# A gated linear recurrence followed by a multiplicative feed-forward: masks, the exchanged v, and the quarters of the array

## The chip, the core and the metric

The kernel runs on one core of one Trainium2 chip. The metric is device time in microseconds (us) for the whole program. The engines are named as in the profile: PE is TensorE (PEld its weight loads), DVE is VectorE, ACT is ScalarE, POOL is GpSimd, SP is SyncE, which here only starts DMAs. An L with a number is a line of the kernel before, unless the text says that it is a line of the changed kernel.

## The reference

Per batch and head (4 x 8, 768 positions, 48 values) a state of 48 x 48 decays by `alpha`, takes in `k v`, and is read by `q`. The result, as a matrix of 3072 x 384, goes through a feed-forward whose two input products are multiplied together.

```
for t in range(S):
    state = alpha[:, :, t, :, None] * state + einsum('bhd,bhe->bhde', k[:, :, t], v[:, :, t])
    y[:, :, t] = einsum('bhd,bhde->bhe', q[:, :, t], state)
x = y.transpose(0, 2, 1, 3).reshape(B * S, H * D)          # 3072 x 384
a = x @ w1                                                 # 384 x 1024
b = x @ w2
h = a * b @ w3                                             # 1024 x 1024
out = h @ w_out                                            # 1024 x 384
```

The activations are float32; the weights arrive as 64-bit floats and are converted on the chip.

## The kernel before

**Tiling.** The 24 chunks are 4 batches of 6 chunks of 128 positions. A head's 48 values are padded to 64, so the 8 heads make 4 pairs (`j`), and a pair fills 128 partitions: head 2j lies in rows 0 to 63 (`i = 0`), head 2j+1 in rows 64 to 127 (`i = 1`). TensorE's array is used in parts: a product with 48 or 64 rows and 64 columns takes a quarter of it, named here (row half, column half). Which row half depends on where the operands lie, which column half on the partitions of the result. Plain float32 products appear in the profile as two matmul records each (20 chunks x 8 products are 320 records at L474); transposes and the split products of the feed-forward appear as one.

**Steps.** One loop runs n from 0 to 24. In step n the kernel works on several chunks at once. In the order of the code: stores and loads; `attend_state(n-1)` (what the old state gives to chunk n-1, L474); `scores(n)` (the products of q and k within a chunk, L454 for chunks 0 to 7, L430 from chunk 8 on) and the masks on DVE (L457, L440), which keep the causal half and make `ms`; `transposed(n+1)` (L381 on PE, copies `qkT` on ACT, L383); conversion of weights (L244 to L262); `advance(n)` on POOL; `turn_v(n)` on POOL (L165); `attend(n-1)` (masked scores times v, L485 or L482, and the copies `x` out of PSUM on ACT, L489); `outer(n)` (the state's new part, L393, added on DVE, L403); `decayed(n+2)` (the product of q, k with their decays, `qk`, L359 on DVE); logarithms and decays of later chunks. From step 6 (`FIRST`) on, pieces of the feed-forward's first products (L554, ACT L563, DVE L565 and L602) are put between. Once a batch's chunks are stored, early groups of them are loaded back and split for these products (L521 on ACT, L522 and L524 on DVE).

**Turned chunks.** From chunk 8 on (`TURNED`) the scores of the first 64 source positions against all targets and those of the last 64 sources against the last 64 targets are two products, in different column halves. For the odd head of a pair the halves come out exchanged, so its `v` must have its halves of positions exchanged as well: `turn_v` writes it to one of two buffers `vts`. The part of the result for the first 64 targets needs only 64 rows; it is made by `attend_low`, called for chunk n-1 between the score products of chunk n. The other part is made in `attend`.

**Where results go.** There are 8 PSUM banks, handed out in turn. The two result banks `y[0]`, `y[1]` of a chunk belong to the row halves: head 2j+i of pair j goes to `y[i]`, pairs 0 and 1 to its lower, pairs 2 and 3 to its upper partitions. The two score banks `sc[i]` belong to the row halves as well.

**Order.** A framework orders the instructions on each engine from the order of the code; `after_marks(...)` holds an instruction behind a named earlier one (`("ms", n)`: the last mask of chunk n; `"pool"`: the last marked instruction on POOL). Engines work through their own queue in order. SP starts loads of `kq` (q and k, L151, L152), alpha, weights and the stores; POOL starts the loads of v for chunks 3 to 7 (L157) and small transfers with the decays at chunk ends (L331, L352, L354, L367).

Of the kernel before, what the change touches and what calls it, by code (L numbers as in the profile page):

```python
# [10 lines left out]
FP32 = mybir.dt.float32  # L11
# [37 lines left out]
def kernel(  # L49
# [12 lines left out]
    nc = tc.nc  # L62
    B, H, S, D = q.shape
    C = 128
    DM = H * D
    DF = moe_w1.shape[1]
    NCH = S // C
# [36 lines left out]
    def bank():  # L104
        return ps.tile([C, 512], FP32, tag="bank", name="bank")
# [3 lines left out]
    def after_marks(*names):  # L109
        stack = ExitStack()  # L110
        for x in names:
            stack.enter_context(tc.issue_after(mark[x]))
        return stack
# [45 lines left out]
    def turned(n):  # L159
        return TURNED <= n < N  # L160
# [251 lines left out]
        mark["pool"] = nc.gpsimd.tensor_tensor(Ts[0][:, :, 0:D], st.pop(("T", n - 1)),  # L412
                                               dec[:, :, None].to_broadcast([C, NP, D]), op=ALU.mult).ins

    def attend_low(n, jj, i, half):

        s, w = ds(DP * i, DP), (vts[n % 2] if i else st["v", n])
        h = half * NP // 2 + jj
        nc.tensor.matmul(st["y", n][0][i][ds(DP * half, DP), jj, 0:DP], w[s, h if i else 2 * h, :],  # L419
                         st["ms", n][s, i, h, 0:DP], start=(n % NCH == 0 and jj == 0), stop=True, skip_group_check=True)  # L420

    def turned_scores(n):

        qkT = st["qkT", n]
        sc = [bank().rearrange("p (j c) -> p j c", j=NP) for _ in range(2)]
        for j in range(NP):
            for part in range(2):
                for i in range(2):
                    r, t = ds(DP * i, D), slice(DP * part, C)
                    nc.tensor.matmul(sc[i][ds(DP * (part ^ i), DP), j, t], qkT[r, 0, j, ds(DP * part, DP)],  # L430
                                     qkT[r, 1, j, t], start=True, stop=True)
            if turned(n - 1):
                for i in range(2):
                    attend_low(n - 1, j % 2, i, i ^ (j < 2))
        ms = work.tile([C, 2, NP, C], FP32, tag="ms", name="ms")
        for i in range(2):
            r = ds(DP * i, DP)
            low, high = (keep_turned[r, 0], keep_turned[:, 1]) if i else (keep[r, 0:DP], keep[:, DP:])
            for x, mask, t in ((slice(DP * i, DP * (i + 1)), low, slice(0, DP)), (slice(0, C), high, slice(DP, C))):
                masked = nc.vector.tensor_tensor(ms[x, i, :, t].bitcast(I32), sc[i][x, :, t].bitcast(I32),  # L440
                                                 mask[:, None, :].to_broadcast([x.stop - x.start, NP, DP]),
                                                 op=ALU.bitwise_and)
        ends_of_part1[0] = mark["ms", n] = masked.ins
        st["ms", n] = ms
# [17 lines left out]

    def attend_state(n):
        qkT = st.pop(("qkT", n))

        y = [bank()[:, 0:HP * C].rearrange("p (j c) -> p j c", c=C) for _ in range(2)]
        st["y", n] = y, [(half * HP + j, i, y[i][ds(DP * half, DP), j, :])
                         for j in range(HP) for i in range(2) for half in range(2)]  # L470
        if n % NCH:
            for j, i, to in st["y", n][1]:
                r = ds(DP * i, D)
                nc.tensor.matmul(to, Ts[n % 2][r, j, :], qkT[r, 1, j, :],  # L474
                                 start=(j % HP == 0), stop=False, skip_group_check=True)

    def attend(n):
        (y, heads), ms, vc = st.pop(("y", n)), st.pop(("ms", n)), st.pop(("v", n))
        for j, i, to in heads:
            if turned(n):  # L480
                w = vts[n % 2][:, j, :] if i else vc[:, 2 * j, :]
                nc.tensor.matmul(to[:, DP:], w, ms[:, i, j, DP:], start=False,  # L482
                                 stop=(j % HP == HP - 1), skip_group_check=True)
            else:
                nc.tensor.matmul(to, vc[:, 2 * j + i, :], ms[:, i, j, :], start=(n % NCH == 0 and j % HP == 0),  # L485
                                 stop=(j % HP == HP - 1), skip_group_check=True)
        x = work.tile([C, HP, 2, C], FP32, tag="x", name="x", bufs=4)
        for i in range(2):
            copied = nc.scalar.copy(x[:, :, i], y[i])  # L489
        ends_of_part1[1] = copied.ins  # L490
        x = x.rearrange("p j i t -> p (j i) t")

        to = xd.rearrange("(b h d) t -> b d h t", b=2, d=D)
        for half in range(2):
            later.append((to[half, :, :, ds(n * C, C)], x[ds(DP * half, D)]))

# [232 lines left out]
    for n in range(N + 1):  # L729
        if not 1 < n < FIRST:  # L730
            store()
        if n in loads:
            load_early(loads[n])
        if n != 1 and not 2 < n <= FIRST:
            load_a(n + 5)
        raws = (3, 3, 3, 3, 2, 2, 3, 3)[n] if n < 8 else 4
        for m in (n + 3,) * (n <= FIRST) + (n + 4,) * (n >= FIRST):
            load_kq(m)
            if 2 < n <= FIRST and m == n + 3:
                load_a(n + 5)  # L740
            if 1 < n < FIRST:
                store()
            if n < FIRST - 2:
                fetch(raws)
        if n >= FIRST:
            load_v(n + 2)
        late_state = early_pair(n - 1)
        if n and not late_state:
            attend_state(n - 1)
        if n < N:  # L750
            scores(n)
            if late_state:
                attend_state(n - 1)
        else:
            for j in range(NP):
                for i in range(2):
                    attend_low(n - 1, j % 2, i, i ^ (j < 2))
        transposed(n + 1)
        if n == 1:
            decays(3)  # L760
            load_a(6)
            with after_marks(("e", 3)):
                logs(4)
        if n == FIRST + 1:
            run(2)
        if n < FIRST:
            with after_marks("pool"):
                load_v(n + 2)
        if n - 2 in begin and n > FIRST:
            g, tiles = begin[n - 2]  # L770
            with after_marks(("ms", n), ("qkT", n + 1)):
                split_early(g)
            fill.extend(gate(g, f) for f in tiles)
        if n == FIRST:
            with after_marks("l", ("qkT", n + 1)):
                split_early(0)
            fill.extend(gate(0, f) for f in begin[n - 3][1])
        pieces = ((3, 3, 2, 0) if n > FIRST + 3 else (0, 3, 3, 0))[(n - FIRST) % 4] if n >= FIRST else 0
        if n == 0:
            with after_marks(("qkT", 0)):  # L780
                logs(2)
            decays(2)
            with after_marks(("e", 2)):
                logs(3)
        early, ready = n < FIRST, len(thirds) if n > 2 else n // 2
        marks = (*[("qkT", n + 1)] * (n < N - 1), *[("qk", n + 1), ("ms", n)] * early, *["x3"] * (n - 2 in begin and n > FIRST))
        if n < N - 2 and n != FIRST:
            with after_marks(*marks):
                convert(2 if early else 1, raws)
        advance(n)  # L790
        turn_v(n)
        if n:
            attend(n - 1)
        outer(n)
        if n > FIRST:
            third(ready)
        run(pieces > 0)
        if early:
            with after_marks(*marks):
                convert(1, raws)  # L800
        with after_marks(*[("ms", n)] * (n < 3)):
            decayed(n + 2)
        if not early:
            with after_marks(*[("qkT", n + 1)] * (n < N - 4)):
                logs(n + 4)
        if n == 4:
            load_early(0)
        convert(early and n > 0, raws)
        run(pieces > 1)
        if n:  # L810
            decays(n + 3)
        if n <= FIRST:
            third(ready)
        if 0 < n < FIRST:
            with after_marks(("e", n + 3)):
                logs(n + 4)
        if n == FIRST:
            with after_marks("x3", ("e", n + 3)):
                convert(2, raws)
        elif n < N - 2:  # L820
            convert(n == FIRST - 1 if early else n % 3 == 0, raws)
        if n == FIRST - 1:
            assert len(done) == 2 * KM
        run(pieces > 2)
        if n == N - 3:
            while begun:
                convert(1)
            weights.extend(load_out(j) for j in range(KF))
            fetch(4)
# [92 lines left out]
```

## Time and profile before

| what | us |
|---|---|
| median of 3 runs | 464.5 (464.01 to 464.53) |
| the profiled execution | 462.59 |
| its span, from first to last instruction | 460.9 |
| PE busy in the span | 446.0 |
| DVE busy | 370.6 |
| ACT busy | 270.7 |
| POOL busy | 87.4 |
| mean granted clock of TensorE | 0.999 |

The profiled execution is 1.9 us below the median and 1.7 us longer than its own span. In the profile's view by stretches of time three stages are seen. Up to 57 us PE is busy for 47.95 us, and DMA engines and DVE are occupied most of the time. From 57 to 187 us the chunks' work and pieces of the feed-forward share PE. From 187 us to the end only feed-forward work is left. A busy PE is a modelled figure, since matmuls are pipelined; for a group of matmuls the text goes by the time from the group's first start to the next group's first start.

### The profile page before, as it was taken

To read this page: it belongs to the slowest core of one execution; us is meant where nothing else is said; L and a number is where in the kernel's file an instruction comes from. 1 tells how busy PE (TensorE), PEld (TensorE's weight loads), DVE (VectorE), ACT (ScalarE), POOL (GpSimd) and SP (SyncE) were. 2 spreads that over 40 slices of the span, in tenths; PEclk is the share of its full clock that TensorE was granted. 3 is DMA by queue.
4 is the path that set the end of the run, shared out by engine and by line. 5 is a ranking of instruction groups with operands and counts; after the bars stand their busy time and mean duration, and the time that the engine had idled before them with its cause. 6 is when DMAs were issued, how large, how long until landed. Compare 5 with 4: busy or idle time off the path is not lost.

```text
span 460.9 us, 10654 instructions
## 1 busy us (share of the span) xinstructions
PE 446.0 (97%) x4080; PEld 394.6 (86%) x4080; DVE 370.6 (80%) x600; ACT 270.7 (59%) x507; POOL 87.4 (19%) x171
## 2 busy tenths in 40 slices
PE   4998999899999999999999999999999999999996
PEld 2676699898989988888888888888888999999996
DVE  2897997999979989798999899999537566776671
ACT  4685966667668563787975757566436333343430
POOL 6134332324414370012021010100000000000000
PEclk9999999999999999999999999999999999999999
DMA  9999999989999965436966364521119655665511
GB/s 174 258 215 226 263 216 208 233 208 226 188 225 186 254 153 167 138 102 187 302 193 207 118 172 133 175 70 46 48 51 288 197 151 165 188 186 158 160 53 51
DMA packets 149379, 79.95 MB, mean 173 GB/s; under 512 B 97184, under 2 KB 138784, under 8 KB 149328
## 3 DMA queue, kind: packets, MB, share of 16 engines
q1 hardware_dynamic: 143840, 64.84, 57.0%
q0 software_dynamic: 5488, 14.43, 10.5%
q8 instruction: 32, 0.52, 0.5%
q14 instruction: 19, 0.16, 0.1%
HBM read 57.19 MB, written 22.06 MB: 172 GB/s over the span
## 4 chain that ended last, share of the span: by engine, by line
PE 89%; DVE 6%; issue 2%; ACT 2%; DMA 1%; DVEq 0%; ACTq 0%
PE bank L554 73%; PE bank L381 3%; PE bank L430 3%; PE bank L482 2%; PE bank L474 2%; DVE qk L359 1%; PE bank L393 1%; PE bank L340 1%; PE bank L346 1%; DVE ms L457 1%; PE bank L454 1%; PE bank L343 1%; PE bank L419 1%; PE bank L485 1%; DMA ac<-in_alpha_dram 1%
## 5 line engine op out<-in xcount | busy, mean ns | idle before, releaser
L554 PE MATMUL bank<-x,w 128*128 128x512 f32 (+1 forms) x688 | 162.7, 374 | 1.5 <-ACT qkT L383 1.2
L554 PEld LDWEIGHTS bank<-x,w 128*128 128x128 f32 x688 | 124.8, 188 | 21.3 <-ACT qkT L383 1.5
L554 PE MATMUL bank<-w3o,ab 128*128 128x384 f32 x576 | 100.2, 336 | 0.0
L554 PEld LDWEIGHTS bank<-w3o,ab 128*128 128x128 f32 x576 | 99.9, 188 | 0.2
L554 PE MATMUL bank<-x3b,w 128*128 128x512 f32 (+1 forms) x248 | 71.9, 385 | 0.0
L579 ACT ACTIVATE bank<-bank 128x512 f32<-128x512 f32 (+1 forms) x72 | 41.0, 571 | 33.1 <-PE bank L554 33.1
L554 PEld LDWEIGHTS bank<-x3b,w 128*128 128x128 f32 x248 | 46.4, 188 | 8.3
L628 POOL DMA_DIRECT2D abd<-r x33 | 19.3, 584 | 138.1 <-DVE r L614 116.2
L678 DVE TENSOR_TENSOR ab<-abl,ab 128x1024 fp32r<-128x1024 f32 x24 | 29.4, 1224 | 14.2 <-ACT ab L677 14.2
L383 ACT COPY qkT<-bank 128x512 f32<-128x512 f32 x48 | 26.1, 599 | 23.1 <-PE bank L381 23.1
L563 ACT ACTIVATE t<-bank 128x384 f32<-128x384 f32 x24 | 11.8, 493 | 45.9 <-PE bank L554 45.9
L677 ACT ACTIVATE ab<-abl 128x1024 fp32r<-128x1024 f32 x24 | 25.5, 1062 | 21.8 <-PE bank L554 19.8
L554 PE MATMUL bank<-wo,w3T 128*128 128x384 f32 x192 | 36.3, 337 | 0.0
L554 PEld LDWEIGHTS bank<-wo,w3T 128*128 128x128 f32 x192 | 34.1, 188 | 1.2
L565 DVE SCALAR_TENSOR_TENSOR o<-bank,t 128x384 f32<-128x384 f32 x24 | 13.4, 558 | 26.1 <-issue 14.3
L249 ACT ACTIVATE power<-power,rebias 128x512 uint32<-128x512 uint32 (+1 forms) x36 | 25.2, 701 | 15.0 <-DVE power L248 14.7
L359 DVE TENSOR_TENSOR qk<-kq,e 128x768 f32<-128x768 f32 x24 | 23.2, 965 | 10.5 <-ACT e L350 7.7
L565 DVE SCALAR_TENSOR_TENSOR r<-bank,r 128x384 f32<-128x384 f32 (+1 forms) x40 | 22.9, 578 | 8.5 <-ACT r L563 5.0
L563 ACT ACTIVATE r<-bank 128x384 f32<-128x384 f32 (+1 forms) x40 | 20.8, 524 | 14.7 <-PE bank L554 12.5
L614 DVE TENSOR_TENSOR r<-bank,r 128x512 f32<-128x512 f32 x32 | 21.9, 684 | 9.2 <-PE bank L554 7.7
L679 DVE SCALAR_TENSOR_TENSOR ab<-ab,abl 128x1024 fp32r<-128x1024 f32 x24 | 29.2, 1218 | 0.0
L251 DVE SCALAR_TENSOR_TENSOR mant<-mant,raw 128x512 f32<-128x512 uint32 (+1 forms) x36 | 23.5, 652 | 2.6 <-ACT raw L244 2.6
(115 smaller groups left out, 741.7 us busy)
## 6 DMA issues: line engine op xcount, KB each, us to landing
abl<-abd SPq DMA_DIRECT2D x24, 512.0 KB, 4.2
abd<-r POOLq DMA_DIRECT2D x33, 256.0 KB, 3.5
raw<-in_moe_w_dram SPq DMA_DIRECT2D x64, 128.0 KB, 3.7
raw<-in_moe_w_dram SPq DMA_DIRECT2D x12, 512.0 KB, 5.9
kq<-in_k_dram SPq DMA_DIRECT2D x24, 192.0 KB, 5.0
kq<-in_q_dram SPq DMA_DIRECT2D x24, 192.0 KB, 5.4
xd<-x SPq DMA_DIRECT2D x48, 96.0 KB, 3.7
xT<-xd POOLq DMA_DIRECT2D x6, 768.0 KB, 5.3
```

What stands on the lines that cost most here:

```text
L249: nc.scalar.activation(power, power, AF.Relu, scale=2.0 ** 23, bias=rebias)
L251: nc.vector.scalar_tensor_tensor(mant, top, 2.0 ** -20, rest, op0=ALU.mult, op1=ALU.add)
L359: mark["qk", n] = nc.vector.tensor_mul(qks[n % 3][:, :, :, 0:D], st.pop(("kq", n)), st.pop(("e", n)).rearrange("p i (h d) -> p i h d", h=H ...
L383: mark["qkT", n] = nc.scalar.copy(qkT[:, :, :, ds(DP * half, DP)], tp[half]).ins
L554: nc.tensor.matmul(p, w[part][i], x[part][i], start=start and part == parts[0] and i == 0, stop=stop and part == parts[-1] and i == n - 1, ...
L563: nc.scalar.activation(t, p1, AF.Copy, scale=(1.0 + 1.0 / P) * scale)
L565: nc.vector.scalar_tensor_tensor(to, p2, scale, t, op0=ALU.mult, op1=ALU.add)
L579: nc.scalar.activation(p, p, AF.Copy, scale=1.0 + 1.0 / P)
L614: nc.vector.tensor_mul(r[0], p, r[0])
L677: nc.scalar.activation(t[:, 0], ab, AF.Copy, scale=1.0 - 2.0 ** -13)
L678: nc.vector.tensor_sub(t[:, 1], ab, t[:, 0].bitcast(FP32))
L679: nc.vector.scalar_tensor_tensor(t[:, 2], t[:, 0].bitcast(FP32), -1.0 - 1.0 / P, ab, op0=ALU.mult, op1=ALU.add)
```

## The change

Three things are changed.

1. In steps 3, 4 and 5 the product of q, k with their decays, `decayed(n + 2)`, is held behind the masks of the step, as it was already in steps 0 to 2.
2. `load_v(n + 2)` of the early steps comes after `advance(n)`; `turn_v` is called for chunk n+1 at the end of step n and no longer for chunk n within step n.
3. From chunk 8 on, the result banks no longer belong to row halves but to target positions: `y[0]` takes the last 64 targets of all heads, `y[1]` the first 64. `attend_state` makes 16 products with 64 targets each where it made 8 with 128; its four quarters are used in turn. `attend_low` always uses the quarters (i, 1-i), while before it used (i, 1-i) for pairs 0 and 1 and (i, i) for pairs 2 and 3. The scores lie as before: 128 targets in (i, i), 64 in (i, 1-i). The result is copied out by three copies: two of 64 partitions from `y[1]`, which move it to the other half of the partitions and are issued ahead of the products of `attend`, and one of 128 partitions from `y[0]`. Before there were two of 128 partitions. The store follows the new order of heads; its pieces keep their size.

```diff
-    def attend_low(n, jj, i, half):
-        s, w = ds(DP * i, DP), (vts[n % 2] if i else st["v", n])
-        h = half * NP // 2 + jj
-        nc.tensor.matmul(st["y", n][0][i][ds(DP * half, DP), jj, 0:DP], w[s, h if i else 2 * h, :],
-                         st["ms", n][s, i, h, 0:DP], start=(n % NCH == 0 and jj == 0), stop=True, skip_group_check=True)
+    def attend_low(n, j, i):
+        s, w = ds(DP * i, DP), (vts[n % 2][:, j, :] if i else st["v", n][:, 2 * j, :])
+        nc.tensor.matmul(st["y", n][1][ds(DP * (1 - i), DP), j, :], w[s], st["ms", n][s, i, j, 0:DP],
+                         start=(n % NCH == 0 and j == 0), stop=(j == NP - 1), skip_group_check=True)
...
             if turned(n - 1):
                 for i in range(2):
-                    attend_low(n - 1, j % 2, i, i ^ (j < 2))
+                    attend_low(n - 1, j, i)
...
     def attend_state(n):
         qkT = st.pop(("qkT", n))
+        if turned(n):
+            y = st["y", n] = [bank()[:, 0:NP * DP].rearrange("p (j c) -> p j c", c=DP) for _ in range(2)]
+            if n % NCH:
+                for j in range(NP):
+                    for t in range(2):
+                        for i in range(2):
+                            r = ds(DP * i, D)
+                            nc.tensor.matmul(y[t][ds(DP * (i ^ t), DP), j, :], Ts[n % 2][r, j, :],
+                                             qkT[r, 1, j, ds(DP * (1 - t), DP)],
+                                             start=(j == 0), stop=False, skip_group_check=True)
+            return
...
     def attend(n):
...
+        if turned(n):
+            x = work.tile([C, NP, C], FP32, tag="x", name="x", bufs=4)
+            for i in range(2):
+                nc.scalar.copy(x[ds(DP * i, DP), :, 0:DP], y[1][ds(DP * (1 - i), DP)])
+            for j in range(NP):
+                for i in range(2):
+                    nc.tensor.matmul(y[0][ds(DP * i, DP), j, :], vts[n % 2][:, j, :] if i else vc[:, 2 * j, :], ms[:, i, j, DP:],
+                                     start=(n % NCH == 0 and j == 0), stop=(j == NP - 1), skip_group_check=True)
+            copied = nc.scalar.copy(x[:, :, DP:], y[0])
...
-        if n < FIRST:
-            with after_marks("pool"):
-                load_v(n + 2)
...
         advance(n)
-        turn_v(n)
+        if n < FIRST:
+            with after_marks("pool"):
+                load_v(n + 2)
         if n:
             attend(n - 1)
         outer(n)
...
-        with after_marks(*[("ms", n)] * (n < 3)):
+        with after_marks(*[("ms", n)] * (n < FIRST)):
             decayed(n + 2)
...
+        turn_v(n + 1)
         run(pieces > 2)
```

With this, the order on the engines differs as follows. On DVE two of the products L359 (the seventh and the eighth of 24) stand behind the two masks of their step and behind three instructions of a weight conversion, in place of ahead of them. On POOL the second v load stands ahead of one small store of decays (L352), and the fourth v load behind `advance` (L412) and no longer ahead of it; the copies of `turn_v` keep their place but for a few neighbours. On ACT the two new copies stand ahead of the `qkT` copies (L383) of the step. On PE only the groups named above change; the order of all others is the same to the end.

More of the change, by code (lines that the diff above doesn't have):

```diff
@@ L477, in attend @@
     def attend(n):
[L478 to L482, printed above, removed]
-                                 stop=(j % HP == HP - 1), skip_group_check=True)
[L484 to L489, printed above, removed]
+        y, ms, vc = st.pop(("y", n)), st.pop(("ms", n)), st.pop(("v", n))
+        to = xd.rearrange("(h i d) t -> i d h t", i=2, d=D) if turned(n) else xd.rearrange("(b h d) t -> b d h t", b=2, d=D)
+        if turned(n):
[7 more added lines that the diff above has]
+            copied = nc.scalar.copy(x[:, :, DP:], y[0])
+        else:
+            y, heads = y
+            for j, i, o in heads:
+                nc.tensor.matmul(o, vc[:, 2 * j + i, :], ms[:, i, j, :], start=(n % NCH == 0 and j % HP == 0),
+                                 stop=(j % HP == HP - 1), skip_group_check=True)
+            x = work.tile([C, HP, 2, C], FP32, tag="x", name="x", bufs=4)
+            for i in range(2):
+                copied = nc.scalar.copy(x[:, :, i], y[i])
+            x = x.rearrange("p j i t -> p (j i) t")
         ends_of_part1[1] = copied.ins
-        x = x.rearrange("p j i t -> p (j i) t")
-        to = xd.rearrange("(b h d) t -> b d h t", b=2, d=D)
         for half in range(2):
@@ L756 @@
                 for i in range(2):
-                    attend_low(n - 1, j % 2, i, i ^ (j < 2))
+                    attend_low(n - 1, j, i)
         transposed(n + 1)
```

## The prediction, made before the changed kernel was run

> **What bounds the kernel now.** I read the page's busy times first (PE 97 per cent, DVE 80), then the chain of waits, then each stage by windows, because an average over the span hides which engine sets a stage. In the chain (start, duration, engine, line), after 187.11 one PE entry of 270 us runs to the last result:
>
> ```profile
> 39.95 0.24 DVE qk L359
> 40.83 1.28 DVE ms L457 x2
> 46.19 0.96 DVE qk L359
> 57.00 3.32 PE bank L554 x18
> 79.21 1.19 ACT x L521
> 187.11 270.22 PE bank L554 x1362
> ```
>
> So whatever moves PE's start on that last stretch moves the end by as much. Ahead of it the bound changes hands. Windows between 80 and 187 us (from:to, length, then busy time of PE, PEld, DVE, ACT, POOL):
>
> ```profile
> 80.40:94.60 14.20, 13.01 (x234) 11.82 (x223) 14.11 (x25) 10.57 (x26) 4.58 (x7) 1.00 0.89 218
> 121.70:138.80 17.10, 17.04 (x297) 15.62 (x301) 13.89 (x30) 11.32 (x26) 4.06 (x9) 1.00 1.08 219
> 138.80:151.00 12.20, 12.20 (x217) 11.07 (x207) 12.09 (x23) 9.43 (x24) 4.94 (x8) 1.00 0.92 187
> 151.00:187.00 36.00, 35.23 (x562) 30.79 (x561) 31.68 (x62) 17.83 (x39) 11.80 (x19) 1.00 0.68 182
> ```
>
> DVE is full in the first and third (steps 10, 11 and 18, 19; so it is up to 116 us), PE in the second and, nearly, in the fourth. In a stretch that DVE fills, a shorter product on PE only makes PE wait longer for a mask.
>
> **Part 1, masks ahead of L359 in steps 3 to 5.** The timeline of DVE and SP:
>
> ```profile
> 36.68 0.69 DVE L253 TENSOR_TENSOR mant<-mant,power 128x512 f32<-128x512 f32 x1
> 39.95 0.96 DVE L359 TENSOR_TENSOR qk<-kq,e 128x768 f32<-128x768 f32 x1 [2.58 <-ACT raw L244]
> 45.57 1.50 SPq L152 DMA_DIRECT2D kq<-in_q_dram  x1
> 51.75 0.95 DVE L359 TENSOR_TENSOR qk<-kq,e 128x768 f32<-128x768 f32 x1
> ```
>
> DVE idles 2.58 us ahead of the L359 at 39.95. The page names ACT, but the q load issued at 33.37 lands 6.1 us later, at 39.4: the wait is for the transfer, with the masks queued behind. Moved ahead, they start when L253 ends, at 37.4 and not 40.83; in the next step at about 44.9 and not 47.15. L276, L262, L245 and L248, and on PE the transposes and products that wait for the masks, go forward. But L359 itself cannot: the q of the ninth chunk is issued at 45.57 and lands 5.2 us later, at 50.78, and L359 starts 0.1 to 1.0 us behind its landing in all steps here, so it moves from 51.75 to about 51.0. The DMA engines are 99 per cent taken between 15 and 70 us, so no load comes earlier for it. I take 0.65 us at 57.0. Bounds: +1.5, if the loads, which wait for freed `kq` buffers, also start sooner; -0.65, if L359, now behind two masks and three conversions (1.28 + 3 x 0.65 = 3.23), is late for its transposes by what these exceed the idle 2.58.
>
> **Part 2, v.** POOL's queue holds the same instructions but for two v loads that change place with one small store and one L412; POOL is 19 per cent busy. `turn_v` lands in the same place. Zero, covered by POOL's idle time; without it, one L412's delay for a load used more than a step later.
>
> **Part 3, PE.** Step 12 (group's first start, duration):
>
> ```profile
> 98.39 0.67 PE L474 MATMUL bank<-qkT,T 48*64 48x128 f32 x16
> 98.88 0.38 PE L430 MATMUL bank<-qkT 48*64 48x128 f32 x7
> 99.23 0.22 PE L419 MATMUL bank<-ms,v 64*64 64x64 f32 x1
> ...
> 100.09 0.28 PE L381 MATMUL bank<-ident,qk 64*128 64x64 f32 x2
> ```
>
> L474 takes 0.49 us to the first L430 (98.88), scores with low products 1.21 (98.88 to 100.09). Within a quarter one pass costs 0.109 us for 128 targets and 0.058 for 64. Pairs 0 and 1, whose low products go into the emptier quarters (i,1-i), take 0.23; pairs 2 and 3, with 0.109 x 2 + 0.058 x 2 in quarter (i,i), take 0.30 to 0.34. All pairs at 0.233 (4 x 0.058 in (i,1-i), beside 2 x 0.109 in (i,i)): 4 x 0.233 + 0.1 = 1.03, so -0.18 to -0.19. The state is 32 passes of 64 over four quarters: 8 x 0.058 = 0.46 each, where it was 4 x 0.109 = 0.44; so 0.49 x 0.46/0.44 = 0.515: +0.025. That 16 starts follow at 15 ns each is seen in the last step, where four quarters run with 64:
>
> ```profile
> 186.09 0.22 PE L419 MATMUL bank<-ms,v 64*64 64x64 f32 x1
> 186.15 0.22 PE L419 MATMUL bank<-ms,v 64*64 64x64 f32 x2
> 186.20 0.22 PE L419 MATMUL bank<-ms,v 64*64 64x64 f32 x2
> 186.27 0.22 PE L419 MATMUL bank<-ms,v 64*64 64x64 f32 x1
> ```
>
> There the change costs: no scores fill the other quarters, so two quarters take all of it, 0.39 to 0.55: +0.16. Total: 13 steps x 0.165 + 2 steps without state x 0.19 - 0.16 = 2.37 us less. Bounds: the low products can't save more than 0.19 a step, since pairs 0 and 1 take 0.23 already, nor less than nothing while the quarters run side by side; the state costs between 32 starts x 0.015 = 0.48 (-0.01) and the third rival's 0.93.
>
> The Trainium skill (TensorE: Matmul & The Clock Gate, section "Wait — 56ns, not 53.3ns?") gives start-to-start as N over 2.4 GHz plus 2.5 ns when warm, 29 ns for N = 64 alone. If starts were serial at that pace, the state would be an estimated 32 x 29 ns = 0.93; the 15 ns starts above, in four quarters, contradict a common pace.
>
> **What is kept of it.** Steps 10 to 15 and 18, 19 are set by DVE. At 94.73, 138.35, 144.07 and 149.72 a feed-forward product waits for the bank that a mask frees (its group takes 3.44 to 3.62 us, not 3.32). There the gain goes into PE's wait. Step 9 passes 0.1 us on through L383 and L521 to DVE's full stretch. Kept: step 16, 0.165; 17, 0.1; 20 to 23, 4 x 0.165; last, -0.16: about 0.75 beside step 9's 0.1. DVE's stretches themselves move with their start, at 80.4.
>
> **Part 3, ACT.** Two copies of 64 partitions x 256 and one of 128 x 256 take the place of two of 128 x 256 (two are 0.64). By that, +0.32 of ACT a step, which has 2.2 us of wait for the transposes L381 ahead of a lone L383. The two early copies need only the low products, which end as L381 starts; L381 takes 0.64 to 0.65, so they just fit: delay 0.05 at most.
>
> **Sum.** 0.65 + 0.1 + 0.75 = 1.5 us, less up to 0.05. Against the profiled execution: 462.6 to 461.1 (span 460.9 to 459.4). That execution lies 1.9 below the median; the same difference on the median of 464.5 gives **463.0 us**. A difference of 0.2 per cent, 0.93 us, is about what a measurement of this kernel can tell.
>
> **Rivals.**
>
> *All of PE's cut is kept* (0.14): DVE's locks are looser than I read, since DVE too moves when scores come sooner. 464.5 - 0.65 - 2.4 = 461.4. For it: PE is at 12.20 of 12.20 us at 138.8 to 151. Against it: DVE is at 12.09, and at 80.4 to 94.6 at 14.11 of 14.20.
>
> *Everything is absorbed* (0.15): the loads at 99 per cent hold the ninth L359 at 51.7, and DVE holds the rest: 464.2.
>
> *The two row halves take turns at a bank* (0.13). In the kernel before each row half writes to its own bank; now both write to `y[t]`, in different partitions. No row here has two row halves in one bank. Were they one after the other, the state would have 16 passes x 0.058 = 0.93 for the 0.44 of now, +0.49 in 14 steps: +6.9, of which PE's idle time at 80.4 to 94.6 (1.2) takes some; 464.5 + 6.9 - 1.2 = 470.2. The low products, in the shadow of the scores, would add little. Against it: two column halves in one bank (L482) run at full pace. The Trainium skill (TensorEngine Tiling (Array Packing), section "Gotcha 1: PSUM Pressure") says that different row tiles cannot access the same PSUM bank simultaneously; that is this mechanism, and no run here shows it yet.
>
> *ACT becomes the bound, slower* (0.14). The early copies stand ahead of L383 in ACT's queue. If the low products end later than a pair of copies (0.64) before the transposes end, or a piece of the conversions is between, L383 slips by up to 0.65. It decides where the scores have little slack behind L383: 0.9, 1.1, 0.6 and 0.4 us in steps 10, 14, 18, 22, and at step 9 where L521 follows L383 at once:
>
> ```profile
> 78.25 1.07 ACT L383 COPY qkT<-bank 128x512 f32<-128x512 f32 x2 [2.21 <-PE bank L381]
> 79.21 1.18 ACT L521 ACTIVATE x<-x3b 128x1152 fp32r<-128x1152 f32 x1
> ```
>
> L521 feeds the DVE stretch. With 0.65 in steps 9, 14, 18 and 22: 464.5 - 1.5 + 4 x 0.65 = 465.6.
>
> **Numbers.** Forecast 0.44; its own range is 462.2 to 464.2 (early part 0 to 1.5, PE part 0.3 to 1.4), six sevenths of it faster. Faster: 0.38 + 0.14 = 0.52. Same: 0.06 + 0.15 = 0.21. Slower: 0.13 + 0.14 = 0.27. The range, 460.9 to 466.2, takes in all but the rival of the bank and tails of the others, about 0.2.
>
> **What would show it.** Right: masks at 37.4 and about 45 us, no DVE idle at 37 to 40, the ninth L359 still at 51; PE's L554 group at 57.0 moves to about 56.3; DVE's first L522 from 80.4 to 79.7; scores with low products 1.03 and the state 0.515; the long PE stretch starts at 185.6. Wrong: state groups near 0.9 (bank), L383 starting behind a copy and not behind L381 (ACT), L554 at 57.0 unmoved (loads), or a start of the long stretch below 185 (PE's cut kept).

## The result and the profile after

| | before | after |
|---|---|---|
| median | 464.5 us (462.66 to 466.18, 6 runs) | 470.03 us (466.82 to 471.44, 6 runs) |
| ratio after / before | | 1.0119, 95% interval 1.0092 to 1.0147 |
| the profiled execution, its span | 462.59, 460.9 | 471.44, 469.7 |
| start of PE's last stretch | 187.11 | 195.75 |
| mean granted clock of TensorE | 0.999 | 0.993 (0.989 to 0.993 in the six runs) |

The changed kernel is slower by 1.2 per cent, some 5.5 us, where 1.5 us less was forecast. The profiled execution is one of its longer ones: the span grew by 8.8 us. L numbers of the changed kernel are by 12 larger from the feed-forward on (L554 is L566, L563 is L575, L565 is L577); L474 is L471, L430 is L429, L419 is L418, L440 is L439, L482 is L493.

The chain of waits of the changed kernel (start, duration, engine, line):

```profile
56.99 3.32 PE bank L566 x18
...
166.84 4.24 DMA dec<-ends
171.60 0.78 POOL dec L411
173.04 0.59 POOL vt L165
...
195.75 270.43 PE bank L566 x1362
```

The last stretch of PE is as long as before (270.43 and 270.22 us) and starts 8.6 us later, so all but 0.2 us of the loss lies ahead of it. The first piece at 57 us starts when it did, so none of the 0.65 us that was forecast for the early part is there. And in place of PE, DVE and ACT the chain now runs over a transfer of decays and POOL's copies of the exchanged v.

The array's parts did what was worked out for them. PE's timeline of step 12 of the changed kernel (a group's first start, its duration):

```profile
98.25 0.69 PE L471 MATMUL bank<-qkT,T 48*64 48x64 f32 x32
98.77 0.39 PE L429 MATMUL bank<-qkT 48*64 48x128 f32 x8
...
99.81 0.72 PE L381 MATMUL bank<-ident,qk 64*128 64x64 f32 x16
```

The state takes 98.25 to 98.77, 0.515 us in the finer starts, and the scores with the low products 98.77 to 99.81, 1.04 us, where it was 1.21. The forecast had 0.515 and 1.03. So two row halves that write into one bank in different partitions run side by side here: one after the other, the state would have taken an estimated 0.93 us.

What was lost is seen near 170 us. POOL's timeline, the kernel before:

```profile
161.50 1.40 POOL L367 DMA_DIRECT2D dec<-ends  x2 [5.42 <-issue]
162.95 1.62 POOL L165 COPY vt<-v 64x192 f32<-64x192 f32 x2
166.77 0.94 POOL L410 TENSOR_TENSOR dec<-dec 128x4 f32<-128x4 f32 x1 [2.20 <-DMA dec<-ends]
```

and the changed kernel, first POOL, then PE's own lines:

```profile
166.14 1.39 POOL L367 DMA_DIRECT2D dec<-ends  x2 [4.32 <-issue]
171.22 0.30 POOL L410 TENSOR_TENSOR dec<-dec 128x4 f32<-128x4 f32 x1 [3.69 <-DMA dec<-ends]
172.45 2.40 POOL L165 COPY vt<-v 64x192 f32<-64x192 f32 x4
```

```profile
170.56 0.28 PE L418 MATMUL bank<-ms,v 64*64 64x64 f32 x2
173.67 0.36 PE L418 MATMUL bank<-ms,vt 64*64 64x64 f32 x1 [2.84 <-POOL vt L165]
```

Before, POOL used the time of the decay transfer to make the exchanged v of chunk 21, and then waited in L410. Now the copies stand behind L410, wait for a transfer that they have no need of, and PE's low products wait for them 2.84 us. The stall is paid for twice. Windows of the changed kernel (the eighth number is the granted clock):

```profile
171.00:173.60 2.60, 0.00 (x0) 0.00 (x0) 2.60 (x5) 0.73 (x2) 2.20 (x4) 0.81 0.66 176
173.60:176.00 2.40, 2.33 (x50) 2.21 (x52) 2.40 (x5) 0.53 (x2) 1.71 (x4) 0.50 0.70 210
176.00:178.00 2.00, 2.00 (x40) 1.88 (x38) 0.71 (x2) 1.65 (x4) 0.34 (x1) 0.50 0.00 0
178.00:180.00 2.00, 2.00 (x13) 1.63 (x10) 1.68 (x4) 0.52 (x2) 1.09 (x3) 0.63 0.20 48
180.00:182.00 2.00, 2.00 (x11) 1.59 (x10) 1.14 (x3) 1.12 (x2) 0.00 (x0) 1.00 0.98 238
```

From 173.6 to about 179.5 PE works at half its clock, which costs it an estimated 3 us more (half of 5.9). Between step 21's state (162.39 and 165.45) and step 23's (176.72 and 185.30) the delay against the kernel before grows from 3.1 to 8.6 us. The first 3 us had come up between 107 and 141 us. There PE idles four times, 2.85 us in all: 0.67 and 0.69 us for ACT's `r` (L575), 0.98 and 0.51 us for masks (L439). In the same steps of the kernel before it idles once, 0.24 us. ACT's `r` in turn waits for the stores of earlier `r`, 16.8 us in all from 57 to 190 us (2.2 before, at L563).

### The profile page after: what moved, and what is told of

Read it like the earlier page. It is cut to its first block, busy times and chain, and to the rows that moved or that the text cites. A ratio compares the mean times of both kernels' runs of the same rounds, so it can differ in the third digit from the quotient of the medians.

```text
span 469.7 us, 11116 instructions
## 1 busy us (share of the span) xinstructions
PE 447.9 (95%) x4304; PEld 396.3 (84%) x4304; DVE 370.4 (79%) x600; ACT 277.6 (59%) x523; POOL 83.8 (18%) x171
## 4 chain that ended last, share of the span: by engine, by line
PE 72%; DMA 13%; issue 4%; DVE 4%; ACT 3%; POOL 1%; SPq 1%; POOLq 0%; ACTq 0%; DVEq 0%
PE bank L566 65%; DMA abd<-r 4%; DMA dec<-ends 3%; DMA ends<-e 3%; DMA ac<-in_alpha_dram 2%; DMA kq<-in_q_dram 1%; PE bank L429 1%; DVE ms L439 1%; PE bank L381 1%; DVE qk L359 1%; PE bank L493 1%; PE bank L343 1%; PE bank L471 1%; ACT e L349 1%; ACT r L575 1%
## 5 line engine op out<-in xcount | busy, mean ns | idle before, releaser
L566 PE MATMUL bank<-x,w 128*128 128x512 f32 (+1 forms) x688 | 162.8, 375 | 0.9 <-ACT r L575 0.5
L566 PEld LDWEIGHTS bank<-x,w 128*128 128x128 f32 x688 | 125.3, 188 | 20.5 <-ACT r L575 0.8
L566 PE MATMUL bank<-w3o,ab 128*128 128x384 f32 x576 | 100.2, 336 | 0.0
L566 PEld LDWEIGHTS bank<-w3o,ab 128*128 128x128 f32 x576 | 99.9, 188 | 0.2
L566 PE MATMUL bank<-x3b,w 128*128 128x512 f32 (+1 forms) x248 | 72.0, 386 | 0.0
L566 PEld LDWEIGHTS bank<-x3b,w 128*128 128x128 f32 x248 | 46.3, 188 | 8.7 <-ACT bank L591 0.5
L575 ACT ACTIVATE t<-bank 128x384 f32<-128x384 f32 x24 | 11.8, 493 | 45.5 <-PE bank L566 45.5
L575 ACT ACTIVATE r<-bank 128x384 f32<-128x384 f32 (+1 forms) x40 | 20.3, 514 | 29.2 <-DMA abd<-r 16.8
L566 PE MATMUL bank<-wo,w3T 128*128 128x384 f32 x192 | 36.3, 337 | 0.0
L566 PEld LDWEIGHTS bank<-wo,w3T 128*128 128x128 f32 x192 | 34.1, 188 | 1.2
L577 DVE SCALAR_TENSOR_TENSOR r<-bank,r 128x384 f32<-128x384 f32 (+1 forms) x40 | 23.0, 578 | 14.3 <-ACT r L575 11.8
L577 DVE SCALAR_TENSOR_TENSOR o<-bank,t 128x384 f32<-128x384 f32 x24 | 13.4, 557 | 25.0 <-issue 14.3
L249 ACT ACTIVATE power<-power,rebias 128x512 uint32<-128x512 uint32 (+1 forms) x36 | 25.1, 696 | 10.6 <-DVE power L248 10.6
L359 DVE TENSOR_TENSOR qk<-kq,e 128x768 f32<-128x768 f32 x24 | 23.4, 976 | 9.8 <-ACT e L350 8.1
L383 ACT COPY qkT<-bank 128x512 f32<-128x512 f32 x48 | 25.8, 588 | 7.2 <-PE bank L381 7.0
```

What stands on the lines that cost most here:

```text
L249: nc.scalar.activation(power, power, AF.Relu, scale=2.0 ** 23, bias=rebias)
L359: mark["qk", n] = nc.vector.tensor_mul(qks[n % 3][:, :, :, 0:D], st.pop(("kq", n)), st.pop(("e", n)).rearrange("p i (h d) -> p i h d", h=H ...
L383: mark["qkT", n] = nc.scalar.copy(qkT[:, :, :, ds(DP * half, DP)], tp[half]).ins
L566: nc.tensor.matmul(p, w[part][i], x[part][i], start=start and part == parts[0] and i == 0, stop=stop and part == parts[-1] and i == n - 1, ...
L575: nc.scalar.activation(t, p1, AF.Copy, scale=(1.0 + 1.0 / P) * scale)
L577: nc.vector.scalar_tensor_tensor(to, p2, scale, t, op0=ALU.mult, op1=ALU.add)
```

## The experiments

Each ratio is to runs of the kernel before on the same chip (median 462.8 to 464.2 us there).

| run | edit | median us | ratio (95% interval) |
|---|---|---|---|
| e1 | changed kernel, exchanged v put ahead again | 466.51 | 1.0056 (1.0032 to 1.0081) |
| e2 | third part alone | 468.18 | 1.0099 (1.0062 to 1.0136) |
| e3 | first part alone | 466.16 | 1.0041 (1.0013 to 1.0068) |
| e4 | second part alone | 462.69 | 0.9984 (0.9961 to 1.0007) |
| e5 | third part, exchanged v ahead | 465.48 | 1.0018 (0.9992 to 1.0044) |
| e6 | first part, scratch buffers | 465.81 | 1.0022 (0.9997 to 1.0047) |
| e7 | before, scratch buffers | 463.61 | 0.9985 (0.9957 to 1.0012) |
| e8 | parts two and three, exchanged v ahead | 464.60 | 1.0002 (0.9974 to 1.0029) |
| e9 | first part, v load later | 464.39 | 1.0032 (1.0011 to 1.0052) |
| e10 | masks of step 4 alone | 464.07 | 1.0035 (1.0015 to 1.0055) |
| e11 | masks of step 5 alone | 462.66 | 0.9993 (0.9976 to 1.0009) |
| e12 | as e8, scratch buffers | 462.84 | 0.9993 (0.9975 to 1.0011) |
| e13 | first part, v load at its old time | 463.00 | 1.0011 (0.9989 to 1.0033) |
| e14 | before, v load early | 463.97 | 1.0035 (1.0014 to 1.0057) |
| e15 | as e12, early copies late | 462.86 | 1.0007 (0.9988 to 1.0026) |
| e16 | second part, scratch buffers | 462.53 | 0.9990 (0.9971 to 1.0008) |
| e17 | changed kernel, both places on POOL | 466.23 | 1.0041 (1.0015 to 1.0068) |
| e18 | changed kernel, v load at its old time | 471.09 | 1.0125 (1.0077 to 1.0174) |

### The place of the exchanged v (e1, e2, e4, e5)

e1 holds the decay products of `advance(n)` behind the copies of `turn_v(n - 1)`. This moves two pairs of copies on POOL, those of chunks 13 and 21, and nothing else on any engine.

```diff
 def turn_v(n):
...
-                nc.gpsimd.tensor_copy(out=vts[n % 2][ds(DP * half, DP), :, 0:D],
-                                      in_=st["v", n][ds(DP * (1 - half), DP), 1::2, 0:D])
+                mark["vt", n] = nc.gpsimd.tensor_copy(out=vts[n % 2][ds(DP * half, DP), :, 0:D],
+                                      in_=st["v", n][ds(DP * (1 - half), DP), 1::2, 0:D]).ins
...
 def advance(n):
-        nc.gpsimd.tensor_mul(dec, d[:, 0, :], d[:, 1, :])
+        with after_marks(*[("vt", n - 1)] * turned(n - 1)):
+            nc.gpsimd.tensor_mul(dec, d[:, 0, :], d[:, 1, :])
```

> The changed kernel, with the copies of turn_v for chunks 13 and 21 held ahead of the decay products of advance(14) and advance(22) on POOL, as they stood in the kernel before; every other instruction on every engine stays in the changed kernel's order. Theory POOL (the exchanged v stands behind a wait for a decay transfer, PE idles 2.84 us in step 22 and then gets a lower clock): most of the loss from 170 us on goes, the clock returns to 0.999, and the time is 465 to 467. Theory ACT (the two early copies hold up ACT's queue and with it the feed-forward's buffers): the stall in step 22 goes but some 3 us of delay built up between 107 and 141 us stay, 467 to 468. Theory loads (the early part makes the transfers some 1 us late from 50 us on): 467 to 468 too, and the early steps look as in the changed kernel.

e2, e4 and e5 are the kernel before with the third part alone, with the second alone, and with the third and e1's edit.

> The kernel before with the third part alone (state in 64s, low products in quarters (i,1-i), three copies). Theory POOL: the two pairs of turn_v copies also stand behind advance here, so as slow as the changed kernel, 469 to 471, clock near 0.99. Theory ACT: the same, 469 to 471, with ACT's r waiting some 15 us for its buffers. Theory loads: the first 57 us are those of the kernel before, the delay of 1 us in the transfers is absent, and the time is 464 to 467.

> The kernel before with the second part alone; on the engines only two v loads on POOL change place. Theory loads: the v load that comes some 2 us earlier takes the DMA engines from the k and q loads of chunk 8, which land 1 to 2 us later, as in the changed kernel (49.2 to 51.1 and 50.8 to 51.7): 465 to 466.5. Theories POOL and ACT: 464.5, no difference.

> The third part alone, with the copies of turn_v held ahead of the decay products as in the kernel before. Theory POOL (what the third part costs is the place of the exchanged v on POOL): the 2.84 us stall of PE near 170 us is gone, and the time is 463 to 465. Theory ACT (the two early copies ahead of qkT cost too): some 2 us stay, 465.5 to 467, and ACT's r still waits more than 10 us for its buffers.

Of the 1.19 per cent, 0.63 go in e1. POOL and PE of e1 in step 22 (L numbers by one larger from L165 on):

```profile
167.31 0.72 POOL L165 COPY vt<-v 64x192 f32<-64x192 f32 x2
172.27 0.68 POOL L411 TENSOR_TENSOR dec<-dec 128x4 f32<-128x4 f32 x1 [4.23 <-DMA dec<-ends]
```

```profile
171.60 0.39 PE L430 MATMUL bank<-qkT 48*64 48x128 f32 x8
...
172.64 0.71 PE L381 MATMUL bank<-ident,qk 64*128 64x64 f32 x16
```

The copies are done at 168.0, POOL waits afterwards, and scores with low products take 1.04 us at full clock. e2 has the same stall (168.12 to 170.96) and 1.0099, e5 has it not and 1.0018. So the place of the copies costs what theory POOL says, and the third part causes it: the order of code for `turn_v` that the second part changes moves no copy at all (in e4 only two v loads change place, and the time is that of the kernel before). The third part doesn't touch `turn_v`. Presumably the framework orders POOL by estimated times, and the other products and copies shift these enough that `advance` seemed ready first; the runs show the new order and not its reason.

One sign of theory POOL did not come: the clock did not return to 0.999. In e1's eight runs it is 0.989 to 0.996. Its trace has another stall, near 89 us, on ACT and then on PE:

```profile
89.29 0.52 ACT L324 ACTIVATE la<-ac 128x384 f32<-128x384 f32 x1 [3.67 <-DMA ac<-in_alpha_dram]
90.25 2.93 PE L567 MATMUL bank<-x,w 128*128 128x384 f32 x8 [2.19 <-ACT r L576]
```

ACT waits 3.67 us for an alpha load, the `r` behind it comes late, PE idles 2.19 us, and the granted clock is 0.50 up to about 93.4. The same kernel without the masks (e8, below) has no stall of PE over 1 us between 57 and 190 us.

### The masks (e3, e6, e7, e9, e10, e11)

```diff
-        with after_marks(*[("ms", n)] * (n < 3)):
+        with after_marks(*[("ms", n)] * (n < FIRST)):          # e3; e10: n < 3 or n == 4; e11: n < 3 or n == 5
             decayed(n + 2)
```

> The kernel before with the first part alone (masks ahead of L359 in steps 3 to 5). My forecast of this part was 0.65 us less, 463.8. Theory loads: the transfers after 48 us become 0.3 to 1 us later and the time is 465 to 466.5. Theories POOL and ACT: between 463.5 and 464.8.

DVE's timeline of e3:

```profile
37.33 1.28 DVE L457 TENSOR_TENSOR ms<-bank,keep 128x512 int32<-128x512 int32 x2
...
43.63 0.36 DVE L403 TENSOR_TENSOR T<-bank,T 128x192 f32<-128x192 f32 x1 [2.13 <-POOL T L412]
...
45.83 1.28 DVE L457 TENSOR_TENSOR ms<-bank,keep 128x512 int32<-128x512 int32 x2
...
52.72 0.96 DVE L359 TENSOR_TENSOR qk<-kq,e 128x768 f32<-128x768 f32 x1 [1.54 <-ACT qkT L383]
```

The first masks start where the forecast put them (37.33 for 37.4), the next at 45.83 and not at 44.9. DVE's idle time ahead of L359 falls from 2.58 to 0.65 us, and 2.13 us come back at L403, which waits for POOL's L412 and so for the transfer `dec<-ends`. And the L359 of chunk 8 is not at 51.0 but at 52.72: its q landed at 52.60 (50.78 before). The waits of ACT between 57 and 190 us (engine, line, releaser: us, times, longest), before and then e3:

```profile
ACT r L563 <- DMA abd<-r: 2.2, 3, 1.1
ACT la L324 <- DMA ac<-in_alpha_dram: 2.1, 1, 2.1
```

```profile
ACT r L563 <- DMA abd<-r: 11.8, 7, 2.6
ACT la L324 <- DMA ac<-in_alpha_dram: 5.3, 3, 4.1
```

SP's loads and stores are 1 to 2.5 us later from 48 us on. ACT waits for them in order, and what PE and DVE need stands behind. To see which wait carries it, e6 and e7 give the second factor of an early feed-forward piece, which is never stored, two buffers of its own.

```diff
-            r.append(gw.tile([C, width], FP32, tag="g", name="r"))
+            r.append((work.tile([C, width], FP32, tag="g2", name="r2", bufs=2) if r
+                      else gw.tile([C, width], FP32, tag="g", name="r")))
             exact(r[-1], *factor, scale)
```

> The first part alone, and the second factor r of the early feed-forward pieces, which is multiplied into the first and never stored, gets two buffers of its own, so that the four buffers of before serve the stored factor only. Theory stores (the transfers are 1 us late, so the stores of r on SP end late, and ACT's r waits 11.8 us for their buffers): the wait of ACT's r for the stores goes to about 0, and the time falls by 1.5 to 2.5 from 466.2, to no more than 0.5 above the kernel before with the same buffers. Theory loads (it is the late q and k themselves, through L359 on DVE): the wait goes, and 1.5 to 2 us above the kernel before with the same buffers stay.

> The kernel before with the two buffers for the second factor r alone. ACT's r waits 2.2 us there for the stores: theory stores gives 0 to 1 us less, 462.7 to 463.7; theory loads no difference.

The wait of `r` for stores is gone in both, and e6 still lies 0.37 per cent above e7, as e3 lies 0.41 above before. Their intervals overlap, so this alone is not clear. But the wait doesn't go with the time in the other runs either: it is 1.9 us in e10 with 1.0035, and 14.5 us in e8 with 1.0002. So theory loads fits better than theory stores. One way is seen in e6, ACT and the windows (granted clock as above), as it was in e1:

```profile
91.05 0.52 ACT L324 ACTIVATE la<-ac 128x384 f32<-128x384 f32 x1 [3.21 <-DMA ac<-in_alpha_dram]
```

```profile
91.00:92.00 1.00, 0.00 (x1) 0.00 (x1) 0.02 (x1) 0.95 (x3) 0.54 (x1) 1.00 0.95 181
92.00:93.00 1.00, 1.00 (x4) 1.00 (x5) 1.00 (x2) 1.00 (x3) 0.00 (x0) 0.64 0.95 187
93.00:94.00 1.00, 1.00 (x5) 1.00 (x4) 1.00 (x3) 1.00 (x3) 0.00 (x0) 0.50 1.05 305
```

ACT stands 3.21 us in L324 for an alpha load, the `r` behind it frees a bank late, PE idles 2.44 us, and the clock falls to a half. It is not the only way: the profiled execution of e3 has such a wait of 4.1 us and no stall of PE over 1.2 us.

What the masks release is seen on POOL, in the kernel before and then in e3:

```profile
46.21 0.53 POOL L354 DMA_DIRECT2D ends<-e  x1 [2.25 <-ACT e L350]
46.73 0.92 POOL L157 DMA_DIRECT2D v<-in_v_dram  x1
```

```profile
44.06 0.53 POOL L354 DMA_DIRECT2D ends<-e  x1
44.59 0.92 POOL L157 DMA_DIRECT2D v<-in_v_dram  x1
```

With the masks ahead, ACT waits for DVE's weight conversion 0.30 us in place of 4.33 (L249), so its decays (L350) are done some 4 us sooner. POOL's small store L354 then waits for nothing, and the v load of chunk 7 behind it starts 2.1 us sooner.

e10 and e11 part the two steps, and e9 sends POOL's v load of chunk 7 later, behind the next small store (issue at 49.97).

```diff
-        if n < FIRST:
+        if n < FIRST - 1:                                      # e9
             with after_marks("pool"):
                 load_v(n + 2)
...
             decays(n + 3)
+        if n == FIRST - 1:
+            with after_marks("pool"):
+                load_v(n + 2)
```

> The first part alone, with the v load of chunk 7 on POOL behind the next small store of decays (issue at about 51 us; 46.7 in the kernel before, 44.6 with the first part); no other instruction changes its place. Theory v (the first part lets POOL issue this v load 2.1 us earlier, and on full DMA engines it overtakes the k and q loads of chunk 8 and the stores that the early group x3b waits for): these land at 49.2, 50.8 and 48.3 again, x3b at 53.5, and the time is 463.7 to 465. Theory places (the transfers are late because L359, which frees their buffers, stands later on DVE): 465.5 to 466.5 as with the first part alone.

> The masks ahead of L359 in step 4 alone (the seventh L359). POOL's v load should then come 2 us early as with the whole first part, since POOL's small store waits for ACT's decays of step 4: theory v 465.5 to 466.5, theory places about half of the loss, 464.5 to 465.5.

> The masks ahead of L359 in step 5 alone (the eighth L359). Theory v: no earlier v load, so no loss, 463.7 to 464.7. Theory places: 464.5 to 466, since L359 of chunk 7 goes from 46.2 to 48.3 us, the larger of the two shifts.

The times in these expectations go by a kernel before of some 464 us, and on this chip it takes 462.8, so the ratios are compared. Nearly all of it is step 4 (1.0035, where e3 has 1.0041); the larger shift of L359, in step 5, costs nothing, which speaks against theory places. e9 came out as theory places had it, against theory v. It is still not clear support: k and q of chunk 8 landed at 49.56 and 50.17 and x3b at 53.16, about as in the kernel before, but the next chunk's loads were late in their place (q at 59.99 and alpha at 62.60, before 58.37 and 59.59). That the later v load took the DMA engines from them is read from these landings and not tested by itself.

### The v load by itself (e13, e14)

e13 keeps the first part and delays this load on POOL by fills of a buffer not yet in use; e14 keeps the kernel before and sends it earlier.

```diff
+        if n == FIRST - 1:                                     # e13
+            for _ in range(8):
+                with after_marks("pool"):
+                    mark["pool"] = nc.gpsimd.memset(vts[0], 0.0).ins
...
         outer(n)
+        if n == FIRST - 2:                                     # e14, and not in step 5
+            with after_marks("pool"):
+                load_v(n + 3)
```

> The first part alone, with eight fills of a buffer not yet in use (some 0.26 us each) on POOL between the small store and the v load of chunk 7, so that this load starts at about 46.7 us as in the kernel before and not at 44.6. Theory v: ratio 0.999 to 1.001. Theory order (DVE's and ACT's own sequence in step 4): 1.003 to 1.004 as with the first part alone.

> The kernel before, with only the v load of chunk 7 on POOL ahead of the small store that waits for ACT (issue at about 44 us and not 46.7). Theory v: 1.002 to 1.004, k and q of chunk 8 land 1 to 2 us later, x3b too. Theory order: 0.999 to 1.001.

The v load, the k load of chunk 8 (KB, us from issue to landing) and x3b, in the kernel before, in e14 and in e13:

```profile
46.73 0.92 POOL L157 DMA_DIRECT2D v<-in_v_dram  x1
kq<-in_k_dram SPq DMA_DIRECT2D x1, 192.0 KB, 4.1
48.41 0.37 SPq L512 DMA_DIRECT2D x3b<-xd  x1
```

```profile
44.04 0.93 POOL L157 DMA_DIRECT2D v<-in_v_dram  x1
kq<-in_k_dram SPq DMA_DIRECT2D x1, 192.0 KB, 5.6
49.90 0.37 SPq L512 DMA_DIRECT2D x3b<-xd  x1
```

```profile
46.94 1.08 POOL L157 DMA_DIRECT2D v<-in_v_dram  x1
kq<-in_k_dram SPq DMA_DIRECT2D x1, 192.0 KB, 4.7
48.89 0.37 SPq L512 DMA_DIRECT2D x3b<-xd  x1
```

One load sent 2.7 us sooner, with no other instruction moved, makes the kernel before slower by 0.35 per cent (0.14 to 0.57). From 15 to 70 us the packets of the queue that serves SP's loads alone take 99 per cent of the DMA engines' time. There the v load goes ahead of k (5.6 us in place of 4.1) and of the stores that x3b waits for (49.90, not 48.41). With its old time the masks cost 0.11 per cent, not clear of nothing, though DVE and ACT run in e3's order. So theory v holds for e14; for the masks e13 is consistent with it but its interval reaches 0.33. Which of the late transfers then costs the time, by way of what, stays open.

### What is left of the third part, and both repairs (e8, e12, e15 to e18)

> The second and third parts with the exchanged v ahead of the decay products, and without the first part. Theory POOL with a first part that costs 1.9 by itself: the changed kernel loses its two costs, 462.5 to 464.5. Theory ACT: 465.5 to 467.

> The second and third parts, the exchanged v ahead of the decay products, no first part, and the two buffers of its own for the second factor r: the candidate for the fastest. If the third part's cut on PE (0.165 us a step) is worth something once nothing else holds, 461.5 to 463.5, below the kernel before and below the same buffers alone (0.9985 of it). If DVE and the loads absorb it: 463 to 464.5.

> As e12, with the two copies of 64 partitions behind the qkT copies in ACT's queue, so that they no longer hold it up while they wait for the low products. If these copies take back PE's cut: 0.3 to 0.5 per cent below e12, ratio 0.995 to 0.997. If DVE and the loads absorb the cut: as e12, 0.998 to 1.000.

> The second part alone with the two buffers of its own for the second factor r: 0.9984 and 0.9985 were measured for each alone, each not clear of 1; if both are real and add up, 0.996 to 0.998; if they were chance, 0.999 to 1.001.

e8 and e12 join earlier edits without the masks; e15 holds the two copies of 64 partitions behind `qkT`:

```diff
-            for i in range(2):
-                nc.scalar.copy(x[ds(DP * i, DP), :, 0:DP], y[1][ds(DP * (1 - i), DP)])
             for j in range(NP):
...
+            with after_marks(*[("qkT", n + 2)] * (n + 2 < N)):
+                for i in range(2):
+                    nc.scalar.copy(x[ds(DP * i, DP), :, 0:DP], y[1][ds(DP * (1 - i), DP)])
             copied = nc.scalar.copy(x[:, :, DP:], y[0])
```

ACT's wait for the low products, e12 and e15:

```profile
ACT x L491 <- PE bank L419: 14.0, 11, 2.0
```

```profile
ACT x L496 <- PE bank L419: 3.0, 2, 1.7
```

The copies do hold ACT's queue, 14 us in all, and nothing is gained when they don't: 0.9993 and 1.0007, so the 0.3 to 0.5 per cent that ACT's hold would have been worth are not there. From the tenth chunk's transposes to the last one's PE takes 98.36 us in e12 (67.83 to 166.19), 98.15 in e15, and 98.38 in e16, which has none of the third part. Without the buffers of its own for `r` it is 101.27 in e8 and 99.07 in the kernel before. In these profiles the third part's cut on PE gives no more than 0.2 us of the 2.4. That DVE takes it, as was forecast for its stretches, fits: it is busy for 66 of the 71 us from 80 to 151 in the kernel before and for 65.7 in e8. No run tests it by itself. e4, e7 and e16 lie below 1 by 0.10 to 0.16 per cent, none clear of it; none of these kernels is shown to beat the kernel before.

> The changed kernel with both places on POOL put back: the exchanged v ahead of the decay products (as in e1) and the v load of chunk 7 at its old time (eight fills ahead of it, as in e13). If the two places are all of the loss: 0.998 to 1.002. If the third part's copies on ACT or the masks' order hold a rest: 1.003 to 1.006.

> The changed kernel with the v load of chunk 7 alone at its old time. The stall of PE in step 22 stays: if the costs add, 1.0119 less 0.0035, so 1.006 to 1.010.

e17 and e18 put e13's fills into e1 and into the changed kernel. e18 is as slow as the changed kernel (1.0125, where 1.006 to 1.010 was expected), with the stall of 2.8 us. e17 didn't come down to 1. The second part sends the v load of chunk 6 to behind L412, so the fills began later and the load went out at 48.31 (48.35 in e18), not 46.7: between e13's 46.94 and e9's 49.97. So neither is a clean test, and what the masks cost beside the third part (e1 against e8: 0.5 per cent) is put down to that v load only by e13 and e14, in the kernel before's surroundings. In e1 itself the stall near 89 us is what the trace shows of it, and e17 has at that place 1.28 us and no fall of the clock. This stays open.

## Why the prediction was wrong

**The step that failed** is part 2 of the prediction, "`turn_v` lands in the same place. Zero". The section on the change says of these copies that they keep their place but for a few neighbours, and the prediction gave the neighbours no price: three pairs of the exchanged copies had changed place with the decay products or their transfers, two pairs of them to behind a wait. Priced from the kernel before, this would have been seen: L410 waits 2.2 to 4.3 us for `dec<-ends` each time, and the copies behind it are needed by the low products at once. It was 0.63 per cent, 2.9 us, between the changed kernel and e1, and 0.81 between e2 and e5. That POOL is idle for most of the span, the reason given for zero, did not help: a queue that waits in order passes the wait on to what stands behind. The same section leaves out that the third part changes the order on DVE and SP too, from 104 us on; e5 and e8 have these orders as well and cost nothing that is clear.

**Part 1** was right on the first masks' time and wrong in sign: -0.65 forecast, with +0.65 as the outer bound, and +0.41 per cent, 1.9 us, measured in e3. Its own sign for this came, the group at 57 us unmoved (56.99). The prediction knew that the DMA engines were 99 per cent taken, and asked only whether loads would come sooner. It did not ask which transfer the work moved forward would release. In step 4 it is a v load that isn't wanted for a step, and it goes ahead of k, q and the stores; e14 shows the price of that, and for the masks themselves it is likely and not shown. Parts 1 and 2 together, 1.9 and 2.9 us, make 4.8 of the 5.5 us lost; the rest is within the intervals.

**Part 3 on PE** was right in each size (0.515, 1.04 for 1.03), and the rule that DVE's stretches take the gain fits the runs. The 0.75 us said to be kept were not found: 0.2 at most.

**The rivals.** Row halves that take turns at one bank: refuted, the state would have been near 0.93. By the Trainium skill (TensorEngine Tiling (Array Packing), section "Gotcha 1: PSUM Pressure") they can't use a bank at the same time; in different partitions they ran at 0.515 us for 32 passes. ACT as the bound: its queue is held as feared, 14 us in e12, without a price. Everything absorbed is what e5 and e8 show for the third part once the copies are in place (1.0018 and 1.0002, neither clear of 1). None of the rivals was the one that decided: none had a wait on POOL or a load that comes too soon, and the loss came through POOL's and SP's queues. The upper end of the range, 466.2, had no term for a wait that is moved by the ordering itself.

## What to carry to other kernels

Where a framework orders the queues, an edit on one engine can reorder others: compare every queue, and price each instruction that moved to behind a wait by that wait, not by its own duration. On DMA engines that are full, a transfer that starts sooner than it must is a loss for another; ask what an earlier step releases before counting it as a gain. And a stall of PE of two or three microseconds cost an estimated 1.6 to 2 times its length here, since the clock went with it: 2.78 us and then half the clock for 3.4 us in e18, 2.84 us and 5.9 us in the changed kernel.

## What was not expected of the hardware

PE idle for 2.84 us (changed kernel), 2.44 us (e6), 2.19 us (e1, near 89 us) and 2.01 us (e5, at 83.75) was followed each time by a granted clock of 0.50, for 3 to 6 us of work. Gaps of 1.19 us (kernel before, at 85.69) and 1.45 us (e1, at 81.88) were not. The Trainium skill (TensorE: Matmul & The Clock Gate, section "Part 1: The HAM clock gate (the "warmup" mystery)") puts the idle time that brings the half clock at some 3.4 us; here 2.01 us were enough. The 32 passes of the state (two for each of 16 products) start 15 ns apart on average (0.476 us from the first to the last): four within 20 ns, and the next four mostly 58 ns after them.
